# Recurrent attention and a GELU layer: v cast by its DMA, the first loads let go in another order, and a newly searched list of steps

## The chip, the cores and the metric

The kernel runs on one core of a Trainium2 chip. The metric is device time in microseconds of one execution; lower is better. The engines are named as the profile names them: PE (TensorE, matrix products; PEld is its weight loads), DVE (VectorE), ACT (ScalarE), POOL (GpSimd) and SP (SyncE). [...]

## The reference

First a gated recurrence, for 4 batches, 8 heads, 768 steps and a head size of 48, then a dense layer with a GELU in the middle over all 3072 tokens:

```python
for t in range(S):
    state = alpha[:, :, t, :, None] * state + np.einsum('bhd,bhe->bhde', k[:, :, t], v[:, :, t])
    y[:, :, t] = np.einsum('bhd,bhde->bhe', q[:, :, t], state)
x = y.transpose(0, 2, 1, 3).reshape(B * S, H * D)          # 3072 x 384
h = x @ w_in                                               # 384 x 2048
g = 0.5 * h * (1.0 + np.tanh(c * (h + 0.044715 * h * h * h)))
out = g @ w_out                                            # 2048 x 384
```

Inputs and output are float32.

## The kernel before, in words

**Tiling.** The 768 steps are cut into 6 chunks of 128. A *unit* is one chunk of one batch: 128 rows of 8 heads by 48, which is 384 columns. A *pair* is two units of the same chunk, batches 0 and 1 or 2 and 3. Pairs 0 to 11 run in order of time; pairs 0 and 1 are both of the first chunk and carry no state in. A step of pair m is named by its kind, the pair, and a number: `kp0.0` is the first `kp` of pair 0.

**Attention of one pair.** `ln` takes the logarithm of alpha (ACT). `cum` sums it over the rows by products with a triangle of ones (PE). `b` and `binv` are the exponentials of plus and minus the sums, `bend` that of the total (ACT). `qp` = q times b and `kp` = k times binv (DVE, line 460). `t` turns qp or kp by PE products with the identity, and `ev` copies the turned tile out (DVE or ACT). `attn` is k times q (PE, line 552), `mask` cuts it to the lower triangle (DVE, line 571), `y` multiplies by v (PE). `x` copies y out, `tx` turns it, `xe` copies it into xT, the input of layer 1. `kv` and `st` make the next state. In pairs 0 and 1 (`PACKED`) the rows of alpha, q and k lie in memory order of another shape, so kp must be turned back for `kv`: those are `t0.4`, `t0.5`, `t1.4` and `t1.5`, with an `ev` each.

**Dense layers.** Layer 1 of one pair is eight blocks `l1m.n`, each of six products of 128 x 256 columns into one bank of PSUM (line 658), each followed by a `gelu` (ACT). Layer 2 (`l2m.n`) is four steps of four products for each unit (line 677), then `ot` copies the result out and `store` sends it (SP).

**Loads.** The rows of pairs 0 and 1 come by twelve *ring loads* of 192 KB on the hardware queues, load.0 to load.11 in the order of `RINGS`; `BY_ACT` says which of them ACT issues, SP issues the rest. POOL issues everything else in the order of `LOADS`: v of pairs 0 and 1 (load.12 and load.14 before), the parts of W_in and W_out, and the rows of later pairs. A `gate` is a small POOL copy that waits for a load and so holds back what POOL issues behind it (line 352). For the pairs in `NARROW`, v comes as float32 and is cast to bf16 by `vb` (line 427); for the others the DMA casts.

**What sets the order.** A scheduler in the kernel holds one list of steps for all engines, `FIRST`. Each entry names an engine and a step (P is PE, V is DVE, A is ACT, G is POOL, S is SP). Each engine runs its own entries strictly in the order of the list; a step waits for what it needs, and all behind it on that engine wait too. `P:fill.n` puts n products of zeros on PE (line 327). `LANDED` holds times at which the scheduler takes the first loads to have landed, by name of the load; it enters no instruction. Tiles come from pools with a fixed number of buffers (`BUFS`): four banks `ff` for layer 1, layer 2 and the sums of pairs 0 and 1, two `yk` for turned tiles, y and kv.

Of the kernel before, what the change touches and what calls it, by code (L numbers as in the profile page):

```python
# [171 lines left out]
class _Kernel:  # L172
# [9 lines left out]
    BY_ACT = (2, 3,)

    FIRST = """
        A:table.0 A:load.2 A:load.3 S:load.0 S:load.1 S:load.4 A:ln0.0 S:load.5 P:fill.7 P:cum0.0 A:ln0.1 G:gate.0 G:load.12 S:load.6 P:cum0.1 A:b0.0
# [2 lines left out]
        P:fill.1 P:t0.4 V:ev0.4 P:fill.1 P:attn0.1 A:ln1.0 G:load.15 P:t0.5 V:mask0.3 P:cum1.0 A:ev0.5 G:load.16 V:vb0.0 A:ln1.1 P:y0.0 V:mask0.2
        G:load.17 P:kv0.0 A:binv1.0 P:cum1.1 V:st0.0 A:x0.0 G:load.18 A:vb0.1 V:kp1.0 P:tx0.0 A:b1.0 P:y0.1 V:xe0.0 G:load.19 V:qp1.0 P:t1.1 A:x0.1
        A:bend1.0 G:load.20 A:b1.1 P:fill.1 P:t1.0 A:ev1.0 V:ev1.1 G:load.21 V:qp1.1 P:fill.1 P:kv0.1 V:st0.1 G:load.22 A:binv1.1 A:bend1.1 P:tx0.1  # L190
        P:attn1.0 V:xe0.1 G:load.23 G:load.24 G:load.25 G:load.26 P:t1.2 P:l10.0 V:kp1.1 V:mask1.0 V:mask1.1 G:load.27 G:load.28 P:t1.3 A:ev1.2
        A:ev1.3 V:vb1.0 P:l10.1 P:t1.4 P:attn1.1 P:y1.0 A:gelu0.0 A:gelu0.1 V:ev1.4 P:l10.2 P:l10.3 A:gelu0.2 P:l10.4 P:t1.5 A:ev1.5 V:vb1.1 V:x1.0
        P:l10.5 V:mask1.2 V:mask1.3 P:y1.1 V:x1.1 P:tx1.0 A:gelu0.3 V:xe1.0 P:l10.7 A:gelu0.4 A:gelu0.7 G:load.29 G:load.30 G:load.31 G:load.32
        P:tx1.1 V:xe1.1 A:gelu0.5 P:l10.6 P:l11.0 A:gelu0.6 P:l11.4 P:l11.3 P:l11.5 A:gelu1.0 A:gelu1.4 A:gelu1.3 P:l11.2 A:gelu1.5 A:gelu1.2 P:l11.7
        A:gelu1.7 P:l11.1 P:l11.6 A:gelu1.1 P:l20.0 A:ln2.0 P:l20.3 P:l20.7 P:cum2.0 P:kv1.0 P:l20.11 P:l20.4 A:b2.0 A:binv2.0 A:ln2.1 P:cum2.1 A:b2.1
        V:st1.0 V:kp2.0 V:qp2.0 P:kv1.1 V:st1.1 G:load.33 G:load.34 G:load.35 G:load.36 G:load.37 V:qp2.1 P:l20.1 G:load.38 P:l20.5 P:l20.8 A:binv2.1
        V:kp2.1 A:gelu1.6 V:tr2.0 V:tr2.1 P:t2.0 A:ev2.1 V:ev2.0 V:tr2.2 V:tr2.3 P:l20.12 G:load.39 G:load.40 G:load.41 G:gate.2 G:load.42 G:gate.3
        G:load.43 G:gate.4 G:load.44 A:ot0.0 P:l20.15 P:attn2.0 A:ot0.3 P:l20.2 V:mask2.2 V:mask2.3 P:l20.9 P:l20.6 A:ln3.0 P:cum3.0 A:b3.0 V:mask2.0
        V:mask2.1 P:y2.0 P:l20.13 V:x2.0 P:y2.1 A:x2.1 V:qp3.0 P:l20.10 P:tx2.0 A:binv3.0 P:tx2.1 A:ot0.1 V:xe2.0 V:xe2.1 P:l20.14 A:ot0.2 P:kv2.0
        V:kp3.0 P:l12.6 P:l12.0 A:gelu2.0 A:gelu2.6 P:l12.5 V:st2.0 P:t3.0 A:gelu2.5 P:l12.1 A:ev3.1 V:tr3.0 P:l12.3 V:tr3.1 V:ev3.0 P:kv3.0 P:l12.7  # L200
        P:kv2.1 A:gelu2.1 P:l12.4 A:gelu2.7 A:gelu2.3 A:gelu2.4 P:l12.2 V:tr3.2 P:l22.4 V:tr3.3 V:st3.0 V:st2.1 P:attn3.0 A:gelu2.2 P:l22.5 P:l22.6
        V:mask3.2 V:mask3.3 A:ln4.0 P:cum4.0 P:l22.0 A:ln5.0 V:mask3.0 V:mask3.1 A:b4.0 P:y3.0 P:l22.7 A:x3.0 P:y3.1 P:kv3.1 V:qp4.0 P:l22.1 A:binv4.0
        A:x3.1 P:l22.2 A:ot2.1 P:tx3.1 V:st3.1 S:store0.0 V:tr4.0 V:xe3.1 P:cum5.0 P:tx3.0 V:xe3.0 V:kp4.0 P:l22.3 P:l13.0 A:binv5.0 A:b5.0 A:ot2.0
        P:l13.3 S:store0.3 P:t4.0 V:tr4.1 V:tr4.2 V:tr4.3 S:store2.1 V:ev4.0 P:l13.4 P:l13.2 V:ev4.1 P:kv4.0 A:gelu3.0 A:gelu3.3 A:gelu3.2 A:gelu3.4
        P:l13.5 A:gelu3.5 G:gate.5 G:load.45 G:gate.6 G:load.46 G:gate.7 G:load.47 G:gate.8 G:load.48 G:gate.9 G:load.49 G:gate.10 G:load.50 G:gate.11
        G:load.51 G:gate.12 G:load.52 G:gate.13 G:load.53 G:gate.14 G:load.54 G:gate.15 G:load.55 G:gate.16 G:load.56 G:gate.17 G:load.57 G:gate.18
        P:kv4.1 P:l13.6 P:l13.1 A:gelu3.6 P:l13.7 V:st4.0 V:st4.1 P:attn4.0 A:gelu3.1 P:l23.0 P:l23.1 A:gelu3.7 S:store2.0 S:store0.1 V:qp5.0 V:tr5.0
        A:ln6.0 V:mask4.2 V:mask4.0 V:mask4.3 V:mask4.1 V:kp5.0 P:l23.2 P:y4.0 P:l23.3 V:ot3.0 S:store3.0 P:y4.1 A:x4.0 A:x4.1 P:cum6.0 P:l23.4 A:b6.0
        P:tx4.0 V:xe4.0 P:tx4.1 V:xe4.1 P:l23.5 A:binv6.0 V:qp6.0 P:t5.0 A:ev5.1 A:ln7.0 V:ev5.0 P:l23.6 P:l23.7 P:attn5.0 P:l14.0 A:ot3.1 V:tr6.0
        V:tr5.1 V:tr5.2 V:mask5.0 S:store0.2 P:l14.4 P:l14.3 V:mask5.1 A:gelu4.0 A:gelu4.4 S:turn6.0 P:l14.6 S:store3.1 A:gelu4.3 A:gelu4.6 V:mask5.2  # L210
        V:mask5.3 P:y5.0 A:x5.0 V:kp6.0 V:tr6.1 V:tr6.2 P:l14.5 V:tr5.3 P:l14.2 A:gelu4.5 A:gelu4.2 P:y5.1 P:l14.1 A:gelu4.1 P:l14.7 P:kv5.1 V:x5.1
        V:tr6.3 P:kv5.0 A:gelu4.7 P:l24.0 P:cum7.0 A:b7.0 A:binv7.0 V:st5.1 P:l24.4 V:st5.0 P:kv6.0 S:turn6.1 V:st6.0 V:qp7.0 P:l24.5 P:l24.1 P:l24.2
        A:ln8.0 P:tx5.0 P:tx5.1 P:cum8.0 V:xe5.1 V:xe5.0 V:kp7.0 A:binv8.0 P:l24.3 V:ot4.0 P:l24.6 A:b8.0 P:l24.7 A:ot4.1 P:attn6.0 V:mask6.0 P:l15.0
        V:mask6.1 P:l15.2 P:l15.4 P:l15.5 V:mask6.2 V:kp8.0 V:mask6.3 P:y6.0 A:gelu5.0 A:gelu5.2 A:gelu5.4 P:l15.6 P:l15.1 V:x6.0 A:gelu5.6 A:gelu5.5
        P:y6.1 V:qp8.0 A:x6.1 S:turn7.0 P:l15.3 P:kv6.1 P:l15.7 A:gelu5.1 P:l25.4 S:turn7.1 P:l25.0 A:gelu5.3 P:l25.5 P:l25.6 A:gelu5.7 A:ln9.0
        V:st6.1 P:attn7.0 P:l25.1 V:mask7.2 P:l25.7 V:mask7.3 G:load.58 G:gate.19 G:load.59 G:gate.20 G:load.60 S:turn6.2 P:l25.2 A:ot5.1 V:mask7.0
        P:cum9.0 A:binv9.0 G:gate.21 G:load.61 G:gate.22 V:mask7.1 V:tr8.0 P:l25.3 P:y7.0 P:y7.1 P:l16.0 V:ot5.0 V:tr7.0 V:tr7.1 A:gelu6.0 A:x7.0
        P:l16.5 P:l16.7 P:l16.3 V:x7.1 S:store4.0 S:turn8.0 P:kv8.1 P:kv8.0 A:gelu6.7 A:gelu6.5 A:gelu6.3 S:turn7.2 V:tr8.1 V:tr8.2 P:l16.6 A:gelu6.6
        P:l16.4 A:gelu6.4 P:l16.1 P:l16.2 A:gelu6.1 A:gelu6.2 V:tr8.3 V:st8.1 V:st8.0 V:tr7.2 V:tr7.3 P:kv7.1 V:st7.1 V:kp9.0 P:kv7.0 P:l26.0 P:l26.1
        P:l26.4 P:l26.5 P:l26.2 S:turn8.1 A:ln10.0 A:b9.0 V:tr9.0 V:tr9.1 V:tr9.2 V:tr9.3 G:load.62 G:gate.23 G:load.63 G:gate.24 G:load.64 G:gate.25  # L220
        V:qp9.0 P:cum10.0 A:binv10.0 P:l26.3 P:l17.0 P:l26.6 P:l26.7 A:ot6.0 A:b10.0 S:turn9.1 A:gelu7.0 P:l17.6 A:gelu7.6 V:ot6.1 V:st7.0 P:l17.1
        A:gelu7.1 P:l17.2 P:l17.3 A:gelu7.2 P:attn8.0 S:turn9.0 V:mask8.0 V:mask8.1 A:gelu7.3 P:l17.7 P:l17.4 A:gelu7.4 A:gelu7.7 P:l17.5 V:mask8.2
        A:gelu7.5 P:l27.0 G:load.65 P:y8.0 V:mask8.3 A:x8.0 P:l27.4 P:y8.1 P:l27.5 P:l27.6 P:l27.1 V:x8.1 V:qp10.0 P:kv9.0 V:kp10.0 A:ln11.0 P:cum11.0
        A:binv11.0 A:b11.0 P:l27.7 P:l27.2 S:turn8.2 P:l27.3 S:store4.1 V:st9.0 P:attn9.0 V:kp11.0 S:store5.1 V:qp11.0 A:ot7.0 A:ot7.1 S:turn10.1
        P:l18.0 S:turn10.0 A:gelu8.0 S:store6.1 P:l18.3 V:mask9.0 V:mask9.1 P:l18.1 A:gelu8.1 A:gelu8.3 P:l18.7 P:l18.5 V:mask9.2 S:turn11.1 V:mask9.3
        P:y9.0 P:y9.1 V:x9.0 V:x9.1 S:store6.2 S:store5.0 S:store6.0 S:turn9.2 S:store7.0 A:gelu8.7 A:gelu8.5 P:l18.2 A:gelu8.2 S:store6.3 P:l18.4
        A:gelu8.4 P:attn10.0 V:mask10.2 V:mask10.3 V:mask10.0 P:l18.6 P:l28.0 P:l28.1 V:mask10.1 A:gelu8.6 P:l28.2 P:l28.3 P:y10.0 P:l19.0 S:store7.3
        S:turn11.0 A:x10.0 A:gelu9.0 P:l19.6 A:gelu9.6 P:y10.1 V:ot8.0 V:x10.1 P:kv9.1 V:st9.1 S:store7.1 P:l19.5 P:l19.3 A:gelu9.5 A:gelu9.3 P:l19.1
# [807 lines left out]
```

## Time and profile before

| | |
|---|---|
| median of 3 runs | 174.1 us (173.99 to 174.16) |
| the profiled execution | 173.77 us |
| its span, first to last instruction | 171.9 us |
| PE busy | 166.3 us (97%) |
| ACT busy | 125.5 us (73%) |
| DVE busy | 107.7 us (63%) |
| POOL busy | 63.0 us (37%) |
| DMA | 29.40 MB, mean 171 GB/s |

Times in the profile are microseconds from the first instruction. A row of a timeline gives the start, the time taken, the engine, the line, the operation and the tiles, with "xN" where N instructions follow each other; the bracket tells how long the engine had been idle and what released it. The chain that ended last is followed back from the last instruction, at each step to what released it. A row of DMA issues gives the tiles, the issuing queue, the count, the size and the median time from issue to landing.

### The profile page before, as it was taken

The page shows a single profiled execution, that of the slowest core. Times are in us where ns is not written, and L with a number is a line of the kernel's source. Part 1 is how long each engine was busy: PE and PEld are TensorE (multiplying, and loading weights), DVE is VectorE, ACT ScalarE, POOL GpSimd, SP SyncE. Part 2 cuts the span into 40 slices and gives each one's busy share as a digit, 9 for nine tenths or more (in the row PEclk, how much of TensorE's full clock was granted, in tenths as well). Part 3 has the DMA queues.
Part 4 walks back from the last instruction along what each step waited for, and adds up shares of the span by engine and source line. Part 5 has one row for each costly group of instructions (what it writes and reads, how often), then busy time and mean ns, then how long its engine had stood idle before and what let it go on. Part 6 is the DMA issues. An engine that isn't in the chain of part 4 may idle for free.

```text
span 171.9 us, 4595 instructions
## 1 busy us (share of the span) xinstructions
PE 166.3 (97%) x1909; PEld 129.8 (75%) x1909; DVE 107.7 (63%) x210; ACT 125.5 (73%) x205; POOL 63.0 (37%) x88
## 2 busy tenths in 40 slices
PE   7999999999999999999999999999999999999991
PEld 2566899666886896797697797796797978987860
DVE  6499820588978999998892898865947550100100
ACT  4578889897999798899779499868882636651412
...
GB/s 138 311 268 217 199 247 230 231 230 228 256 208 96 257 218 241 169 165 242 145 224 213 158 226 138 181 233 60 232 186 148 147 1 114 4 0 40 101 48 92
DMA packets 51541, 29.40 MB, mean 171 GB/s; under 512 B 39616, under 2 KB 47936, under 8 KB 51520
## 3 DMA queue, kind: packets, MB, share of 16 engines
...
q14 instruction: 6, 0.05, 0.1%
...
## 4 chain that ended last, share of the span: by engine, by line
PE 91%; DMA 3%; ACT 3%; DVE 0%; issue 0%; DVEq 0%
PE hT L658 37%; PE acc L677 37%; PE at L552 4%; DMA k<-in_k_dram 3%; PE yps L627 2%; PE cum L416 2%; PE kv L581 2%; PE qkT_ps L484 1%; PE xT_ps L646 1%; PE qkT_ps L470 1%; PE yps L561 1%; ACT qkT L508 1%; PE k_ps L516 1%; ACT L318 1%; PE idle L327 1%; PE yps L617 1%
## 5 line engine op out<-in xcount | busy, mean ns | idle before, releaser
L658 PE MATMUL hT<-xT,w_in 128*128 128x256 bf16 x576 | 69.4, 273 | 0.0
L677 PE MATMUL acc<-w_out,gT 128*128 128x384 bf16 (+3 forms) x416 | 68.9, 314 | 0.0
L664 ACT ACTIVATE gT<-hT 128x512 bf16<-128x512 f32 x96 | 53.6, 600 | 15.2 <-PE hT L658 13.1
L658 PEld LDWEIGHTS <-w_in 128*128 128x128 bf16 x576 | 60.6, 114 | 1.2 <-DMA w_in<-in_moe_w_in_dram 0.3
L677 PEld LDWEIGHTS <-gT 128*128 128x128 bf16 x416 | 37.4, 98 | 20.2
L571 DVE TENSOR_TENSOR atm<-at,ut 128x512 bf16<-128x512 f32 x48 | 30.1, 683 | 8.2 <-PE at L552 8.0
L689 DVE COPY ot<-acc 128x384 f32<-128x384 f32 (+2 forms) x9 | 4.3, 488 | 20.0 <-PE acc L677 20.0
L689 ACT COPY ot<-acc 128x384 f32<-128x384 f32 (+1 forms) x17 | 7.9, 472 | 11.6 <-PE acc L677 9.3
L595 DVE STREAM_TRANSPOSE tr<-b 32x256 f32<-32x256 f32 x32 | 14.0, 438 | 1.4 <-ACT b L449 0.8
L346 POOL DMA_DIRECT2D k<-in_k_dram x11 | 12.2, 1111 | 5.7 <-DMA v<-in_v_dram 1.7
L346 POOL DMA_DIRECT2D a<-in_alpha_dram x11 | 12.3, 1117 | 4.4 <-issue 1.7
L460 DVE TENSOR_TENSOR qp<-q,b 128x768 bf16<-128x768 f32 (+1 forms) x15 | 11.9, 792 | 2.8 <-ACT b L449 2.6
L346 POOL DMA_DIRECT2D vb<-in_v_dram x11 | 12.2, 1105 | 3.6 <-issue 1.9
L346 POOL DMA_DIRECT2D q<-in_q_dram x11 | 12.2, 1112 | 2.5 <-DMA w_out<-in_moe_w_out_dram 1.0
L449 ACT ACTIVATE binv<-cum 128x768 bf16<-128x768 f32 (+1 forms) x15 | 10.1, 684 | 3.3 <-PE cum L416 3.3
L460 DVE TENSOR_TENSOR kp<-k,binv 128x768 bf16<-128x768 f32 (+1 forms) x15 | 11.9, 791 | 0.5 <-ACT binv L449 0.5
L318 ACT ACT_TABLE_LOAD x9 | 11.5, 1283 | 0.9 <-PEq L1020 0.7
L449 ACT ACTIVATE b<-cum 128x768 f32<-128x768 f32 (+1 forms) x15 | 10.3, 685 | 2.0 <-PE cum L416 1.5
L664 ACT ACT_TABLE_LOAD x9 | 11.5, 1283 | 0.2
L606 DVE TENSOR_TENSOR stmp<-kv,st 128x384 f32<-128x384 f32 x16 | 8.9, 555 | 1.9 <-PE kv L581 1.2
L608 DVE TENSOR_TENSOR st<-stmp,tr 128x384 bf16<-128x384 f32 x16 | 8.9, 558 | 0.6
L399 ACT ACTIVATE la<-a 128x768 f16<-128x768 f32 (+1 forms) x11 | 8.5, 784 | 0.1
...
## 6 DMA issues: line engine op xcount, KB each, us to landing
out_dram<-ot SPq DMA_DIRECT2D x19, 192.0 KB, 3.0
...
vb<-in_v_dram POOLq DMA_DIRECT2D x9, 192.0 KB, 6.3
...
w_out<-in_moe_w_out_dram POOLq DMA_DIRECT2D x4, 384.0 KB, 11.0
...
```

The source lines that it names most:

```text
L318: nc.scalar.add_instruction(mybir.InstLoadActFuncSet(name=nc.get_next_instruction_name(), act_func_set_id=i, engine=mybir.EngineType.Activ ...
L346: dma(u[t][:, lo:hi].rearrange("t b h d -> t (b h) d"), src.rearrange("b h s d -> s (b h) d")[c * C:(c + 1) * C])
L449: self.nc.scalar.activation(u[n].rearrange("t i h d -> t i (h d)")[:, lo:hi], cum, AF.Exp, scale=1.0 if n == "b" else -1.0)
L460: self.nc.vector.tensor_tensor(out, rows, b, op=ALU.mult)
L571: self.nc.vector.tensor_tensor(u["atm", i][:, o], u["at", i][o], self.ut[:, None, :].to_broadcast([self.C, self.H // 2, self.C]), op=ALU.mult)
L595: self.nc.vector.transpose(u["tr"][f:f + 32, :, 0:32], rows[:, lo:lo + H * 2 * D].rearrange("t (g n) -> t g n", n=2 * D)[:, :, 0:32])
L606: nc.vector.tensor_tensor(s, acc, old, op=ALU.add)
L608: nc.vector.tensor_tensor(new, acc, end[:, :, None].to_broadcast([C, H // 2, 2 * D]), op=ALU.mult)
L658: self.nc.tensor.matmul(h[:, s].rearrange("p (g t) -> p g t", t=self.C), w_in[:, j, nt % 4 + s], self.xT[c % self.NX][:, lo:hi, j], start= ...
L664: return lambda e: self.nc.scalar.activation(self.gT[c % self.NG][:, nt:nt + 2, lo * self.C:hi * self.C], f.pop(("h", c, lo, nt)), AF.Gelu ...
L677: self.nc.tensor.matmul(f["acc", c, b][:, lo:hi], self.gT[c % self.NG][:, nt, b * self.C:(b + 1) * self.C], self.w_out[:, nt, lo:hi], star ...
L689: self.copy(e)(f["ot", c, b][:, sl], f["acc", c, b] if half is None else f["acc", c, b, half][:, sl])
```

## The change

Five things are edited.

- `NARROW` is empty: v of pairs 0 and 1 comes as bf16 from its DMA, and the four `vb` casts are gone.
- `RINGS` swaps two entries, so that load.4 is now k and load.5 q of pair 0, unit 1. `BY_ACT` leaves load.2 alone to ACT. `LOADS` lets POOL go on from the alpha of pair 0, unit 0 (it was unit 1), drops the gate on k, and puts W_in 1 ahead of the second v.
- `APART`: four of the eight layer-1 blocks of pair 0 (nt 0, 2, 4, 6) are done for one unit first (`h1`, six products of 128 columns) and then for the other.
- Layer 2 no longer has to come after all layer-1 blocks of the first two pairs (`firsts`).
- `FIRST` is a new list from its first entry, and `LANDED` has new times. In the new list 7 products of zeros are left of 17. The ring loads stand in it as A: load.2 and S: load.0, 1, 8, 5, 7, 9, 10, 4, 6, 3, 11.

The edits around `u["apart"]` in `cum` and `exp` are for pairs that take `ff` banks without being packed; there are none.

```diff
-    LOADS = ('gatea 0 1', 'v0', 'gatek 0 1', 'in 0', 'v1', 'in 1', 'in 2', 'in 3', 'out 0', 'out 1', '2a', 'out 2', '2b', 'out 3', '3', '4', '5', 'win3', '6', '7', '8', '9', '10', '11')
+    LOADS = ('gatea 0 0', 'v0', 'in 0', 'in 1', 'v1', 'in 2', 'in 3', 'out 0', 'out 1', '2a', 'out 2', '2b', 'out 3', '3', '4', '5', 'win3', '6', '7', '8', '9', '10', '11')
...
-    RINGS = (('a', 0, 0, 1), ('a', 0, 1, 2), ('q', 0, 0, 1), ('k', 0, 0, 1), ('q', 0, 1, 2), ('k', 0, 1, 2),
+    RINGS = (('a', 0, 0, 1), ('a', 0, 1, 2), ('q', 0, 0, 1), ('k', 0, 0, 1), ('k', 0, 1, 2), ('q', 0, 1, 2),
              ('a', 1, 0, 1), ('a', 1, 1, 2), ('q', 1, 0, 1), ('k', 1, 0, 1), ('q', 1, 1, 2), ('k', 1, 1, 2))
-    BY_ACT = (2, 3,)
+    BY_ACT = (2,)
...
-        A:table.0 A:load.2 A:load.3 S:load.0 S:load.1 S:load.4 A:ln0.0 S:load.5 P:fill.7 P:cum0.0 A:ln0.1 G:gate.0 G:load.12 S:load.6 P:cum0.1 A:b0.0
-        S:load.7 A:bend0.0 V:qp0.0 A:binv0.0 A:binv0.1 S:load.8 V:kp0.0 P:fill.2 P:t0.0 A:b0.1 V:ev0.0 P:fill.1 P:t0.1 S:load.9 A:ev0.1 V:qp0.1
-        S:load.10 A:bend0.1 P:fill.3 P:attn0.0 V:kp0.1 G:gate.1 S:load.11 P:t0.2 G:load.13 V:mask0.0 A:ev0.2 P:t0.3 G:load.14 V:mask0.1 A:ev0.3
...
+        A:table.0 A:load.2 S:load.0 P:fill.7 A:ln0.0 P:cum0.0 S:load.1 S:load.8 S:load.5 S:load.7 A:ln0.1 A:b0.0 G:gate.0 S:load.9 V:qp0.0 A:binv0.0
+        S:load.10 G:load.12 S:load.4 S:load.6 S:load.3 G:load.13 G:load.14 G:load.15 G:load.16 G:load.17 G:load.18 G:load.19 G:load.20 P:cum0.1 A:b0.1
+        P:t0.0 V:kp0.0 A:ln1.0 A:binv0.1 P:t0.1 P:cum1.0 V:ev0.0 V:qp0.1 P:t0.2 V:kp0.1 A:bend0.1 A:bend0.0 A:ev0.1 P:attn0.0 V:ev0.2 A:b1.0 A:binv1.0
+        V:mask0.0 V:mask0.1 P:t0.3 A:ev0.3 P:attn0.1 V:mask0.2 P:y0.0 A:bend1.0 A:ln1.1 A:x0.0 P:cum1.1 S:load.11 P:tx0.0 V:qp1.0 P:t1.0 A:ev1.0
+        A:bend1.1 A:binv1.1 A:b1.1 V:kp1.0 V:xe0.0 V:mask0.3 P:t1.1 V:ev1.1 P:h10.0 P:y0.1 P:h10.3 P:t1.4 P:attn1.0 A:x0.1 P:tx0.1 P:h10.1 A:ev1.4
...
+        P:l211.2 P:l211.3 V:ot11.0 S:store11.0 P:l211.7 P:l211.8 P:l211.9 A:ot11.1 A:ot11.2 A:ot11.3 S:store9.0 S:store11.1 S:store11.3 S:store8.1
+        S:store11.2 P:l210.0 P:l210.4 P:l210.5 P:l210.6 P:l210.7 P:l210.1 V:ot10.1 S:store9.1 S:store10.1 P:l210.2 P:l210.3 A:ot10.0 S:store10.0
...
-    NARROW = (0, 1)
+    NARROW = ()
...
+    APART = (0, 2, 4, 6)
...
-    def layer1(self, f, c, lo, hi, nt):
+    def layer1(self, f, c, lo, hi, nt, units=None):
+        a, b = units or (lo, hi)
...
-                    self.nc.tensor.matmul(h[:, s].rearrange("p (g t) -> p g t", t=self.C), w_in[:, j, nt % 4 + s],
-                                          self.xT[c % self.NX][:, lo:hi, j],
+                    self.nc.tensor.matmul(h[:, s, (a - lo) * self.C:(b - lo) * self.C].rearrange("p (g t) -> p g t", t=self.C), w_in[:, j, nt % 4 + s],
+                                          self.xT[c % self.NX][:, a:b, j],
...
-                t = s.add("l1", {"PE": W["l1_4"]}, 10000 + n, self.layer1(f, c, lo, hi, nt),
-                          [xts[c, b] for b in range(lo, hi)] + [loads["w", "in", nt // 4]], stream=n - 16 if m > 1 else None)
+                h1 = []
+                if m == 0 and nt in self.APART:
+                    h1 = [s.add("h1", {"PE": W["l1_2"]}, 10000 + n, self.layer1(f, c, lo, hi, nt, (lo, lo + 1)), [xts[c, lo], loads["w", "in", nt // 4]])]
+                t = s.add("l1", {"PE": W["l1_2" if h1 else "l1_4"]}, 10000 + n, self.layer1(f, c, lo, hi, nt, (lo + 1, hi) if h1 else None),
+                          [xts[c, b] for b in range(lo, hi)] + [loads["w", "in", nt // 4]] + h1, stream=n - 16 if m > 1 else None)
...
-                          gs[m if m else b // 2][2 * part:2 * part + 2] + [loads["w", "out", min(part, 3)]] + firsts, stream=n - 16)
+                          gs[m if m else b // 2][2 * part:2 * part + 2] + [loads["w", "out", min(part, 3)]], stream=n - 16)
```

More of the change, by code (lines that the diff above doesn't have):

```diff
@@ L181 @@
              ('a', 1, 0, 1), ('a', 1, 1, 2), ('q', 1, 0, 1), ('k', 1, 0, 1), ('q', 1, 1, 2), ('k', 1, 1, 2))
-    BY_ACT = (2, 3,)
+    BY_ACT = (2,)
     FIRST = """
-        A:table.0 A:load.2 A:load.3 S:load.0 S:load.1 S:load.4 A:ln0.0 S:load.5 P:fill.7 P:cum0.0 A:ln0.1 G:gate.0 G:load.12 S:load.6 P:cum0.1 A:b0.0
-        S:load.7 A:bend0.0 V:qp0.0 A:binv0.0 A:binv0.1 S:load.8 V:kp0.0 P:fill.2 P:t0.0 A:b0.1 V:ev0.0 P:fill.1 P:t0.1 S:load.9 A:ev0.1 V:qp0.1
-        S:load.10 A:bend0.1 P:fill.3 P:attn0.0 V:kp0.1 G:gate.1 S:load.11 P:t0.2 G:load.13 V:mask0.0 A:ev0.2 P:t0.3 G:load.14 V:mask0.1 A:ev0.3
[L188 to L228, printed above, removed]
-        S:store8.0 S:turn10.2 A:gelu9.1 P:attn11.0 V:mask11.2 V:mask11.3 P:l19.2 A:gelu9.2 V:mask11.0 V:mask11.1 P:l28.4 P:l28.5 P:l28.6 P:l28.7
-        A:ot8.1 P:y11.1 P:l19.4 P:y11.0 P:l19.7 A:x11.0 A:gelu9.4 A:gelu9.7 V:x11.1 P:l110.0 S:store8.1 P:l110.4 S:turn11.2 S:store7.2 P:l110.3
-        A:gelu10.0 A:gelu10.4 A:gelu10.3 P:l29.4 P:l29.5 P:l29.6 P:l110.2 P:l29.7 V:ot9.1 A:gelu10.2 P:l111.0 P:l111.5 A:gelu11.0 A:gelu11.5 P:l111.7
-        P:l111.3 P:l111.2 P:l111.1 A:gelu11.7 A:gelu11.3 P:l111.6 A:gelu11.2 A:gelu11.1 P:l111.4 P:l211.0 P:l211.1 A:gelu11.4 P:l211.2 A:gelu11.6
-        P:l211.4 P:l211.5 A:ot11.1 P:l211.3 A:ot11.0 P:l211.6 P:l211.7 P:l29.0 P:l29.1 P:l29.2 P:l211.8 P:l29.3 P:l211.9 S:store11.1 V:ot11.2
-        S:store11.2 P:l110.6 V:ot9.0 S:store9.0 P:l110.1 A:gelu10.6 V:ot11.3 S:store11.3 S:store11.0 A:gelu10.1 P:l110.7 P:l110.5 S:store9.1
-        A:gelu10.7 P:l210.4 P:l210.5 P:l210.0 P:l210.1 A:gelu10.5 P:l210.6 P:l210.2 P:l210.7 A:ot10.1 P:l210.3 A:ot10.0 S:store10.1 S:store10.0
@@ new lines @@
+        A:gelu0.5 P:tx1.0 V:xe1.0 G:load.25 G:load.26 G:load.27 G:load.28 P:l10.7 P:tx1.1 P:l10.6 V:xe1.1 A:gelu0.4 A:gelu0.7 A:gelu0.6 P:l11.0
+        P:l11.4 G:load.29 G:load.30 G:load.31 G:load.32 G:load.33 G:load.34 G:load.35 G:load.36 P:l11.7 P:l11.5 P:t1.5 P:t0.5 A:gelu1.0 G:load.37
+        G:load.38 G:load.39 G:load.40 A:gelu1.7 A:gelu1.4 A:gelu1.5 P:l11.1 A:gelu1.1 P:l11.3 A:gelu1.3 P:l11.2 A:gelu1.2 V:ev0.5 V:ev1.5 P:kv1.0
+        P:kv1.1 A:ln2.0 A:ln2.1 V:st1.0 P:l20.0 P:l20.4 V:st1.1 P:kv0.0 V:st0.0 P:kv0.1 V:st0.1 P:l11.6 P:cum2.0 P:l20.8 P:l20.3 A:b2.0 A:binv2.0
@@ L415, in emit @@
                     continue
-                nc.tensor.matmul(cum[:, i, 0:H * D], self.ut_h, la[:, i, :, 0:D], start=True, stop=True)
+                rows = cum[lo] if u["apart"] else cum[:, i]
+                nc.tensor.matmul(rows[:, 0:H * D], self.ut_h, la[:, i, :, 0:D], start=True, stop=True)
                 for p in range(H // 2) if u["sums"] == "PE" else ():
-                    nc.tensor.matmul(cum[:, i, H * D + p:H * D + p + 1],
+                    nc.tensor.matmul(rows[:, H * D + p:H * D + p + 1],
                                      la[:, i, 2 * p:2 * p + 2, :].rearrange("t h d -> t (h d)"),
@@ L447, in emit @@
                     u[n] = self.sb.tile([self.C, 2, H, D], BF16, tag=n, bufs=self.BUFS["binv"], name=n)
-                cum = u["cum"][lo][:, None, 0:H * D] if u["packed"] else u["cum"][:, lo:hi, 0:H * D]
+                cum = u["cum"][lo][:, None, 0:H * D] if u["apart"] else u["cum"][:, lo:hi, 0:H * D]
                 self.nc.scalar.activation(u[n].rearrange("t i h d -> t i (h d)")[:, lo:hi], cum, AF.Exp,
@@ L749, in tasks @@
         for step in self.LOADS:
-            if step[0] == "v":
-                rows(int(step[1:]), "v")
+            if step[0] in "aqkv" and step[1:].isdigit():
+                rows(int(step[1:]), step[0])
             elif step[:4] == "gate":
@@ L801, in tasks @@
             if m in self.CUM_FF:
-                cums[0].take("ff", *exps[:3])
-                cums[1].take("ff", *exps[3:])
+                cums[0].take("ff", *exps[:len(exps) // 2])
+                cums[1].take("ff", *exps[len(exps) // 2:])
             else:
                 cums[0].take("ca", *exps)
-            if m in self.SPLIT:
+            if m in self.SPLIT and m not in self.CUM_FF:
                 cums[1].deps += exps[:2]
@@ L927, in tasks @@
         n = 0
-        f, gs, l2s, ots, parts_of, firsts = {}, {}, {}, [], [], []
+        f, gs, l2s, ots, parts_of = {}, {}, {}, [], []
         def layer1(m):
```

52 lines of the change are left out of this document (46 added, 6 removed), and 9 rows, old and new, of the table LANDED.

## The prediction

> **What bounds the kernel now.** I read the page's busy shares and slices first, then the chain that ended last, then the first microseconds of SP's, TensorE's and VectorE's timelines, then the DMA issues of that stretch.
>
> ```profile
> PE 166.3 (97%) x1909; PEld 129.8 (75%) x1909; DVE 107.7 (63%) x210; ACT 125.5 (73%) x205; POOL 63.0 (37%) x88
> ...
> PE   7999999999999999999999999999999999999991
> ```
>
> TensorE is the bound from the second slice to the last. But its busy time counts products of zeros (line 327), so the early nines are not all work. The chain, in order of time (start, length, what):
>
> ```profile
> 1.92 5.28 DMA k<-in_k_dram
> ...
> 7.29 0.57 DVE kp L460
> ...
> 16.95 0.66 PE hT L658 x6
> ...
> 23.61 5.90 PE hT L658 x54
> ```
>
> Up to 16.8 us the chain is one of latency: it waits for the k rows of pair 0, unit 0 (load.3) until 7.20, and goes through the first pair's attention. From the first layer-1 product on, TensorE has work without a break; beyond 30 us the starts of its products leave only three waits over 0.1 us that are no change of tile shape (at 37.4, 52.5 and 107.5), 0.46 us together. So the time is: when the first layer-1 product starts, plus the TensorE work still undone then, plus a fixed end (last product 168.3, copy 0.48, store, 171.9).
>
> What lets load.3 land at 7.20 is where it stands among the ring loads. SP's issues, then what the issues of 0.7 to 2.0, of 4.9 to 6.1 and of 7.3 to 8.3 us took to land:
>
> ```profile
> 0.73 1.41 SPq L343 DMA_DIRECT2D a<-in_alpha_dram  x2
> 2.20 0.61 SPq L343 DMA_DIRECT2D q<-in_q_dram  x1
> 2.85 0.62 SPq L343 DMA_DIRECT2D k<-in_k_dram  x1
> 3.52 1.27 SPq L343 DMA_DIRECT2D a<-in_alpha_dram  x2
> 4.83 0.61 SPq L343 DMA_DIRECT2D q<-in_q_dram  x1
> 5.49 0.61 SPq L343 DMA_DIRECT2D k<-in_k_dram  x1
> ```
>
> ```profile
> a<-in_alpha_dram SPq DMA_DIRECT2D x2, 192.0 KB, 3.1
> ...
> k<-in_k_dram ACTq DMA_DIRECT2D x1, 192.0 KB, 5.3
> ```
>
> ```profile
> k<-in_k_dram SPq DMA_DIRECT2D x1, 192.0 KB, 5.9
> ```
>
> ```profile
> q<-in_q_dram SPq DMA_DIRECT2D x1, 192.0 KB, 4.5
> k<-in_k_dram SPq DMA_DIRECT2D x1, 192.0 KB, 4.3
> ```
>
> SP issues one load per 0.65 us. The first two landed 3.1 us after issue, those in a backlog 4.3 to 5.9. load.3 was the second issue of ACT's own queue, at 1.92.
>
> **The change, part by part.**
>
> *Ring loads in another order.* In the new list SP issues load.0, 1, 8, 5, 7, 9, 10, 4, 6, 3, 11; ACT only load.2. So load.3 goes from the fourth ring load to the eleventh. SP's first eight issues start at 0.73 to 5.49 as above; the ninth follows at 6.14 and load.3 at 6.80. It lands between 6.80 + 3.05 = 9.85 (an empty queue) and 6.80 + 5.9 = 12.7 (the tenth of before, which met the first v on POOL's queue). I take 11.9: the eleventh of before landed at 7.42 + 4.5 = 11.9, and POOL's loads are no less in the way here, since the new gate waits for the first alpha (3.8) instead of the second (4.8), and the gate on k (POOL idle for 1.80 us until it) is gone, so v0 and W_in are let go up to 3 us earlier, among the ring loads.
>
> Who waits: kp0.0 is VectorE's second product. Behind it on VectorE stand ev0.0, qp0.1, kp0.1 and everything else; on TensorE t0.1, its transpose, stands before the cumulative sums of pair 1 and all that follows. Only cum0.0, cum0.1 and t0.0 go ahead. So kp0.0 moves from 7.29 to 11.9, +4.6 us. load.6 (alpha of pair 1) is issued just before it and lands just before it; the others earlier.
>
> *The new order behind kp0.0.* Before, the first layer-1 product came 9.5 us after kp0.0 (16.79). Now VectorE carries the path: kp .47, ev .60, qp .47, kp .47, ev .60, three masks at .605, qp .47, kp .47 (start to start, from VectorE's timeline), 5.4 us with a short wait; then xe and a transpose of k, 0.6: the first product at 11.9 + 6.05 = 17.95. From there to the first block of pair 1 TensorE has eight layer-1 blocks (8 x .655), three y (.20 each), four transposes (.22), two attn (.33), three tx (.17): 7.9, and 0.2 of waits. That block starts at 26.05; before it started at 23.61 + .66 = 24.27: +1.8. Not done by then, though done before: t0.5, t1.5, kv0.0, kv0.1: 2 x .22 + 2 x .17 = +0.8. Together +2.6.
>
> *Products of zeros.* Ten of 17 go. They stood in waits, 0.22 us each, and cost nothing in the sum above. But without them, and with load.3 late, TensorE stands idle from 6.6 to 12.5. What that does to its pace no row of before shows; these are the nearest:
>
> ```profile
> 1.19 3.17 PE L327 MATMUL idle<-zero 128*128 128x512 bf16 x7 [1.19 <-DVE ones L990]
> 4.37 1.39 PE L384 MATMUL cum<-la,ut_blk 128*128 128x384 f16 x7
> ...
> 5.70 0.82 PE L384 MATMUL cum<-la,ut_blk 128*128 128x384 f16 x7
> ```
>
> After standing, TensorE took 0.42 us from one 512-column product to the next, and started the first cum0 at half pace too, until about 4.9, 3.7 us after its first product; later the same product took 0.22. The granted clock of the page reads full throughout and does not tell the two apart. If TensorE falls back to that pace, t0.1 (.22), cum1.0 (.76) and t0.2 (.22) cost 1.2 us more, of which 1.1 reaches ev0.2 and the masks behind it, and 0.4 follows with t0.3 and attn0.1: +1.5. Ends: 0 (it keeps its pace) and +2.4 (half pace up to the first layer-1 product). I take +1.5: the start of this kernel, a stand followed by sparse work, is the row it is nearest to. [...]
>
> *v cast by DMA.* Four casts go (three of 0.35 on VectorE, one of 0.53 on ACT). On VectorE they were in the latency stretch, which I have counted anew without them. The casting load writes 192 KB in 96-byte pieces; later loads of this kind landed 1.4 to 2.2 us after the one before them, the uncast a, q and k 1.8: -0.4 to +0.4 on POOL's queue. y0.0 needs v0 at 15.9, 4 us after the latest landing I can make of it (it is first of POOL's queue): 0. W_in 0 is needed at 17.95; before it landed at 14.3, two places later on POOL: 0. If the rings were fast again, W_in would be next.
>
> *Four blocks by units.* 48 products of 128 columns (.056 each) take the place of 24 of 256 (.109): +0.07 in all, within the 0.2 of waits.
>
> *The rest of the list; removed dependencies.* The waits beyond 30 us may go or others come: -0.5 to +0.5; I take -0.3, most of the 0.46 us of waits above, whose places the new order does not repeat; the end (l210.3, ot10.0, store10.0) is the same. The edits in cum and exp change no instruction for pairs 0 and 1.
>
> Sum against the profiled execution: 173.77 + 2.6 + 1.5 - 0.3 = 177.6. The median of the runs, 174.1, is 0.3 above it: 177.9.
>
> **The rivals.** A change under 0.2% (0.35 us) can't be told from none here.
>
> *Late k, full pace* (+2.3): 176.4. For it: in all the trace the pace never fell once it was up. Against: there was no stand over 0.5 us in which it could.
>
> *k early.* If the ring loads run at 0.56 us each without losing to POOL's queue, load.3 lands at 9.85 to 10.5: +0.2 to +0.9, around 174.9. For it: SP's loads landed 0.5 to 0.6 us apart from 7.4 to 9.6. Against: the next took 1.8 us more once v0's packets ran.
>
> *Faster.* The shortening behind kp0.0 (9.5 to 6.05 us, less the 0.8 put off) is worth some 2 us if load.3 does not pay for it. The point that decides is its landing: no loss at 9.6, a gain before. At 9.0 the time is 173.5. Against: that is 2.2 us after its issue, and no ring load landed in under 3.0.
>
> *The order does not hold* (SP issuing load.3 early after all) would give 7.3 and 171.8; the instructions stand in the listed order, so it keeps 0.01.
>
> **How the numbers follow.** Late k and half pace 0.50 (177.9), late k at full pace 0.28 (176.4), k early 0.14 (174.9; a third of it within 0.2%), faster 0.07, and 0.01 for the last. The likeliest, by itself, runs from 176.3 (landing 11.0) to 179.8 (13.2, with half pace up to layer 1). The range reaches down through the second and into the third case: 175.2 to 179.8, leaving some 0.12 below and 0.06 above. Faster 0.08, same 0.05, slower 0.87.
>
> **What would show it.** The chain of the changed kernel should begin with a DMA of k until about 11.9, from SP, not ACT; TensorE idle from 6.6 to 12.5 in front of the transposes of kp; transposes and sums behind it at twice their spacing if the pace fell; the first layer-1 product near 18 to 19.5; no wait for W_in behind it. A k that lands before 9.6 would make the forecast wrong, and so would long TensorE waits after 30 us.

## The result and the profile after

| | before | changed |
|---|---|---|
| median | 174.10 us (3 runs) | 183.49 us (182.93 to 184.04, 4 runs) |
| the profiled execution | 173.77 us | 183.54 us |
| its span | 171.9 us | 181.8 us |

The changed kernel takes 1.054 times as long, with a 95% interval of 1.050 to 1.058. The forecast was slower, at 177.9 us in a range of 175.2 to 179.8. So the sign came out, and the chain that was forecast, but the size did not: the time lies 3.7 us above the range. Executions that took over 1.5% longer than the fastest of their kernel are left out of all comparisons, and as the profiles of the two runs named "v uncast" and "old loads, new list" below are of such executions, only their first 30 and 20 us are read.

First the busy shares, the slices of TensorE and the slices of the granted clock of the changed kernel (40 slices of 4.5 us):

```profile
PE 165.7 (91%) x1923; PEld 131.3 (72%) x1923; DVE 112.0 (62%) x215; ACT 120.7 (66%) x196; POOL 62.3 (34%) x87
...
PE   7501899999999999999999999999999999999992
...
PEclk9955569999999999999999999999999999999999
```

TensorE is busy for about as long (165.7 us against 166.3; ten products of zeros fewer, and part of the work at a slower pace) in a span that is 9.9 us longer, and the gap is in the second to fifth slice. Behind them the slices are full, as before. In the third to fifth slice the clock shows 5, which is half, and in the sixth 6. In the kernel before, that row was full throughout:

```profile
PEclk9999999999999999999999999999999999999999
```

The start of the chain that ended last (start, length, what):

```profile
6.84 9.80 DMA k<-in_k_dram
...
16.73 0.57 DVE kp L463
...
17.35 0.61 PE qkT_ps L473 x4
...
25.31 0.59 PE hT L665 x6
```

It is the chain that was forecast: the k rows of pair 0, unit 0 (load.3), issued by SP at 6.84, hold back kp0.0, then t0.1, then cum1.0. But load.3 landed at 16.64, where the forecast had 11.9. TensorE's timeline shows the stand in front of t0.1 and where layer 1 begins:

```profile
17.35 0.61 PE L473 MATMUL qkT_ps<-ident,kp 128*128 128x128 bf16 x4 [10.09 <-DVE kp L463]
17.75 1.49 PE L386 MATMUL cum<-la,ut_blk 128*128 128x384 f16 x7
...
25.10 0.79 PE L665 MATMUL hT<-xT,w_in 128*128 128x128 bf16 x6
```

Busy time of the engines and granted clock in four stretches (PEclk is the column in front of the DMA share):

```profile
core 0: us, PE busy (x) PEld busy (x) DVE busy (x) ACT busy (x) POOL busy (x), PEclk, DMA share, GB/s
0.00:7.00 7.00, 5.35 (x32) 2.70 (x33) 3.26 (x21) 3.58 (x6) 4.28 (x13) 1.00 0.64 185
7.00:17.00 10.00, 0.25 (x4) 0.08 (x2) 0.27 (x1) 1.03 (x4) 5.30 (x7) 0.58 1.41 212
17.00:25.50 8.50, 7.46 (x73) 5.72 (x74) 6.45 (x13) 3.77 (x10) 3.77 (x5) 0.50 1.32 211
25.50:30.00 4.50, 4.50 (x86) 4.20 (x85) 4.10 (x8) 3.80 (x7) 2.26 (x4) 0.98 1.30 234
```

From 17 to 25.5 us everything on TensorE ran at half its clock. The cumulative sum at 17.75 took 1.49 us; before, the same form took 0.82 at 5.70.

The 9.77 us between the two profiled executions, 5.94 of which the sum of the prediction (177.6) did not have, split into three:

| stretch | forecast | measured | off by |
|---|---|---|---|
| kp0.0 starts | 11.9 | 16.73 | 4.83 |
| from kp0.0 to the first layer-1 product | 6.05 + 1.5 = 7.55 | 25.10 - 16.73 = 8.37 | 0.82 |
| from there to the end, more than before | 1.44 - 0.3 = 1.14 | (183.54 - 25.10) - (173.77 - 16.79) = 1.46 | 0.32 |

(The three add up to the 5.94 to rounding. 1.44 is the +2.6 of the late k less the 17.95 - 16.79 = 1.16 by which the first layer-1 product was to move.) What had to be explained was chiefly the 4.8 us of the landing.

### The profile page after: what moved, and what is told of

Read it like the earlier page. It is cut to its first block, busy times and chain, and to the rows that moved or that the text cites. A ratio compares the mean times of both kernels' runs of the same rounds, so it can differ in the third digit from the quotient of the medians.

```text
span 181.8 us, 4611 instructions
## 1 busy us (share of the span) xinstructions
PE 165.7 (91%) x1923; PEld 131.3 (72%) x1923; DVE 112.0 (62%) x215; ACT 120.7 (66%) x196; POOL 62.3 (34%) x87
## 4 chain that ended last, share of the span: by engine, by line
PE 88%; DMA 5%; SPq 3%; ACT 1%; issue 0%; DVE 0%; DVEq 0%
PE hT L665 35%; PE acc L684 35%; DMA k<-in_k_dram 5%; PE at L555 4%; SPq L345 3%; PE yps L630 2%; PE cum L419 2%; PE kv L584 2%; PE qkT_ps L473 2%; PE cum L386 1%; PE xT_ps L649 1%; PE qkT_ps L487 1%; PE yps L564 1%; PE yps L620 1%; PE k_ps L519 0%
## 5 line engine op out<-in xcount | busy, mean ns | idle before, releaser
L665 PE MATMUL hT<-xT,w_in 128*128 128x256 bf16 (+1 forms) x600 | 69.7, 270 | 0.0
L665 PEld LDWEIGHTS <-w_in 128*128 128x128 bf16 x600 | 61.8, 114 | 1.1
L696 DVE COPY ot<-acc 128x384 f32<-128x384 f32 x13 | 7.2, 557 | 21.9 <-PE acc L684 21.3
L463 DVE TENSOR_TENSOR kp<-k,binv 128x768 bf16<-128x768 f32 (+1 forms) x15 | 11.9, 793 | 10.7 <-DMA k<-in_k_dram 9.9
L348 POOL DMA_DIRECT2D vb<-in_v_dram x13 | 14.6, 1122 | 4.1 <-issue 2.6
L696 ACT COPY ot<-acc 128x384 f32<-128x384 f32 (+3 forms) x13 | 5.6, 431 | 13.1 <-PE acc L684 12.3
L348 POOL DMA_DIRECT2D k<-in_k_dram x11 | 12.2, 1111 | 5.9 <-DMA w_out<-in_moe_w_out_dram 2.2
L348 POOL DMA_DIRECT2D a<-in_alpha_dram x11 | 12.2, 1113 | 5.8 <-DMA vb<-in_v_dram 2.1
L348 POOL DMA_DIRECT2D q<-in_q_dram x11 | 12.2, 1108 | 5.2 <-DMA w_in<-in_moe_w_in_dram 2.1
L463 DVE TENSOR_TENSOR qp<-q,b 128x768 bf16<-128x768 f32 (+1 forms) x15 | 11.9, 794 | 3.2 <-ACT b L452 3.1
L640 DVE CAST x<-yps 128x384 bf16<-128x384 f32 x11 | 6.0, 557 | 9.0 <-PE yps L630 5.3
L473 PE MATMUL qkT_ps<-ident,kp 128*128 128x128 bf16 x16 | 2.2, 283 | 10.1 <-DVE kp L463 10.1
```

Source lines behind the costliest of these rows:

```text
L348: dma(u[t][:, lo:hi].rearrange("t b h d -> t (b h) d"), src.rearrange("b h s d -> s (b h) d")[c * C:(c + 1) * C])
L463: self.nc.vector.tensor_tensor(out, rows, b, op=ALU.mult)
L665: self.nc.tensor.matmul(h[:, s, (a - lo) * self.C:(b - lo) * self.C].rearrange("p (g t) -> p g t", t=self.C), w_in[:, j, nt % 4 + s], self ...
L696: self.copy(e)(f["ot", c, b][:, sl], f["acc", c, b] if half is None else f["acc", c, b, half][:, sl])
```

## The experiments

The theory: the place of load.3 in SP's queue costs what was forecast, and the rest of its delay comes from POOL's loads, which now start before the rings are done; the stand of TensorE costs more because the clock falls. Rivals: the ring order is harmless and POOL's traffic alone does it; or the new list is slower in itself; or the casting loads with their 96-byte pieces are to blame.

"Changed" below is the changed kernel; diffs are against it unless said otherwise. Of long lists the entries that move are shown; a gate's own entry in the list, and the loads that stand behind it, move to match and are not shown. The kernel before ran again beside each set of runs, and the ratios are to those.

| run | ratio to before (95%) | load.3 lands | first layer-1 product |
|---|---|---|---|
| changed | 1.054 (1.050 to 1.058) | 16.64 | 25.10 |
| ring order undone | 1.015 (1.010 to 1.021) | 6.57 | 17.09 |
| gate on k behind v0 | 1.041 (1.033 to 1.049) | 13.04 | 21.50 |
| zeros in the stand | 1.041 (1.035 to 1.046) | 16.11 | 22.45 |
| v uncast | 1.094 (1.079 to 1.108) | 19.41 | 29.00 |
| k by ACT | 1.012 (0.997 to 1.026) | 6.96 | 14.17 |
| old loads, new list | 1.012 (0.999 to 1.026) | 6.95 | 14.50 |
| old list, cast | 1.000 (0.995 to 1.006) | 7.04 | 16.84 |
| old list, new ring order | 1.027 (1.011 to 1.044) | 12.36 | 24.11 |
| POOL behind k | 1.024 (1.020 to 1.028) | 10.85 | 18.32 |
| W_in 0 first | 1.006 (1.001 to 1.010) | 7.04 | 15.20 |
| W_in 0 first, zeros | 1.003 (1.000 to 1.007) | 7.37 | 15.76 |

**The ring order undone.** SP issues its ring loads in the order of their numbers; all else is as in the changed kernel.

```diff
- S:load.0 S:load.1 S:load.8 S:load.5 S:load.7 S:load.9 S:load.10 S:load.4 S:load.6 S:load.3 S:load.11
+ S:load.0 S:load.1 S:load.3 S:load.4 S:load.5 S:load.6 S:load.7 S:load.8 S:load.9 S:load.10 S:load.11
```

> The changed kernel with SP's ring loads let go in the order of their numbers (load.0, 1, 3, 4, 5, 6, 7, 8, 9, 10, 11); nothing else differs. Theory (late k of pair 0, and the half clock behind the stand that it makes, are the whole loss): load.3 lands near 6.5, kp0.0 goes at 6.6 to 7.3 as before the change, and what is late next are the q and k of pair 1 (issues 8 and 9 of SP, 13 and 15 us); the first layer-1 product comes near 16.5 and the time is 172.5 to 175.5 us. Rival (the new list or the early weights are slow in themselves, the late k costs little): 180 us or more.

176.68 us (176.30 to 177.12). Undoing the order gives back 6.8 of the 9.4 us, so most of the loss needs it, but that is 1.2 us less than expected. The chain shows what is late next:

```profile
6.14 9.59 DMA k<-in_k_dram
...
15.83 0.56 DVE kp L460
...
17.29 0.64 PE hT L662 x6
```

This k is load.9, of pair 1, unit 0. It has the same fate as load.3 had: issued at 6.14, landed at 15.73, and kp1.0 stands ahead of xe0.0 on VectorE, so layer 1 waits for it. Issued at 6.14 here and at 6.84 in the changed kernel, a ring load took 9.59 and 9.80 us to land.

**A gate on k behind v0.** POOL issues v0, then waits for load.3 before it issues W_in.

```diff
-    LOADS = ('gatea 0 0', 'v0', 'in 0', 'in 1', 'v1', ...
+    LOADS = ('gatea 0 0', 'v0', 'gatek 0 0', 'in 0', 'in 1', 'v1', ...
```

> The changed kernel with one gate more: behind v0 POOL waits for load.3 (k of pair 0, unit 0) before it lets W_in go. Ring order as changed. Theory (W_in's 1024-byte pieces take turns with the ring loads' 768-byte pieces, one for one, from 9 us on, and so hold load.3 back): load.3 lands at 11 to 12.5 instead of 16.6, the stand is 2 to 4 us shorter at least, and the time is 177 to 179.5 us. Rival (the 96-byte pieces of the casting load of v hold it back): they are still there, so load.3 lands at 15.5 or later and the time is 182 us or more.

181.44 us, and load.3 at 13.04: without W_in beside the rings it lands 3.6 us earlier, but later than expected. The time is 2 us above what was expected. From kp0.0 (13.13) to the first layer-1 product it took 8.4 us, as in the changed kernel, so the half clock was paid in full (the sum at 14.15 took 1.49 us); and behind that product the profiled execution takes 2.0 us longer than the changed kernel, of which 1.2 is one wait of TensorE, up to 93.2 us, for a DMA that turns qp (`qkT<-qp`); what held up that DMA stays open. W_in is the larger share of what delays load.3 (3.6 us), v0 a smaller one.

**POOL behind k altogether.** The one gate of POOL waits for load.3 in place of alpha, so that nothing of POOL runs beside the rings.

```diff
-    LOADS = ('gatea 0 0', 'v0', ...
+    LOADS = ('gatek 0 0', 'v0', ...
```

> The changed kernel, ring order as changed, but POOL's one gate waits for load.3 (k of pair 0, unit 0) and not for the first alpha, so that neither v0 nor W_in runs beside the ring loads. Theory (its place as SP's tenth issue costs load.3 only some 3 us behind its issue at 6.8; all above that is POOL's traffic, which takes turns with SP's queue): load.3 lands at 9.9 to 10.8 instead of 16.6, and W_in, let go 5 us later, becomes the late one; 176 to 182 us. Rival (SP's queue is slow by itself with eleven loads in it): load.3 lands at 12 or later.

178.46 us, as expected. Its chain starts so:

```profile
6.79 4.06 DMA k<-in_k_dram
...
10.91 0.18 POOL gate L351
```

load.3 lands at 10.85, 2.2 us before the run with v0 alone beside it. So of its delay against before (7.20), 3.65 us belong to its place in SP's queue, and 5.8 us to POOL's traffic. The DMA queues between 7 and 9 us show the second part directly (packets, MB, and the time that the packets took as a share of 16 engines, 140.7% in one of the rows). First this run, then the changed kernel:

```profile
q1 hardware_dynamic: 777, 0.56, 94.3%
```

```profile
q0 software_dynamic: 1532, 0.15, 140.7%
q1 hardware_dynamic: 278, 0.20, 35.9%
```

q1 is SP's queue, q0 POOL's. Beside the 96-byte pieces of v0 SP moved 0.20 MB instead of 0.56. Then W_in comes on. The changed kernel between 12 and 15 us:

```profile
q0 software_dynamic: 404, 0.39, 77.9%
q1 hardware_dynamic: 404, 0.29, 39.4%
```

404 pieces of one queue beside 404 of the other: while W_in ran, SP got about one piece of 768 bytes for each of POOL's of 1024 (some twenty on each side are shorter). That is 97 GB/s, from which a load of 192 KB is estimated at 2.0 us. The ring loads of the changed kernel landed at 10.63, 13.04, 15.06, 16.64 and 17.60, so 2.4, 2.0, 1.6 and 1.0 us apart, where the four before them were 0.5 us apart (6.48, 7.03, 7.53, 8.04). What the expectations call taking turns is, as measured, these equal counts beside W_in; in what order the two queues were served was not shown. Beside v0 the counts, 1532 and 278, are far from equal, and no run here shows why.

**v uncast.** v of pairs 0 and 1 comes as float32, with the four casts on VectorE; all else is as in the changed kernel.

```diff
-    NARROW = ()
+    NARROW = (0, 1)
...
+ V:vb0.0 V:vb0.1 V:vb1.0 V:vb1.1
```

> The changed kernel with v of pairs 0 and 1 loaded as float32 and cast by VectorE (four casts ahead of the y that needs each). Theory (W_in's turns hold load.3 back, not the cast of v): load.3 lands within 1.5 us of 16.6 and the time is 182.5 to 185 us. Rival (the 96-byte pieces do it): load.3 lands by 13.5 and the time is 180.5 us or less.

190.3 us, and load.3 at 19.41, 2.8 us later than in the changed kernel instead of within 1.5 (read from one profile). That misses the expectation, and goes against the rival still more: the casting loads are not what is wrong. The queues between 7 and 9 us:

```profile
q0 software_dynamic: 91, 0.35, 61.0%
q1 hardware_dynamic: 286, 0.21, 35.7%
```

Beside 91 large pieces of uncast v SP moved 0.21 MB, as it moved 0.20 beside the 1532 small ones, and v brings twice the bytes. In this order of loads v cast by DMA is even the better choice (1.054 against 1.094). Part of the longer time lies behind the landing: the casts stand in front of y0.0 and y0.1 here, with waits of TensorE of 1.05 and 0.41 us for them. The first layer-1 product came 3.9 us later than in the changed kernel, which the 2.8 and the 1.05 make up.

**The cast alone.** The kernel before with the casting loads, and the four `vb` gone from its list (the diff is against before).

```diff
-    NARROW = (0, 1)
+    NARROW = ()
...
- V:vb0.0 A:vb0.1 V:vb1.0 V:vb1.1
```

> The kernel before with one part of the change: v of pairs 0 and 1 cast by DMA, the four casts of VectorE and ACT left out of the list. Theory (the cast itself is hidden): the ring loads land within 0.7 us of before, and the time is 173.3 to 174.6 us. Rival (the casting load's 96-byte pieces hold the ring loads back): k of pair 1 lands 1 us or more later, and the time is 174.8 us or more.

174.86 us, 1.000 (0.995 to 1.006). By the figures alone this is the rival's: the time lies 0.3 us above the theory's range, and the last three ring loads moved from 11.39, 11.88 and 12.32 to 9.89, 12.29 and 13.46, so the last k of pair 1 came 1.1 us later. But the kernel before took 174.73 us beside it, so a ratio of 1.000 is what counts: with the old list and the old gates, any cost of the cast is below 0.6%.

**The ring order alone.** The kernel before with SP's order of the change and load.3 on SP, POOL's gates as they were (the diff is against before, the loads called by the numbers that they have there).

```diff
-    BY_ACT = (2, 3,)
+    BY_ACT = (2,)
...
- S:load.0 S:load.1 S:load.4 S:load.5 S:load.6 S:load.7 S:load.8 S:load.9 S:load.10 S:load.11
+ S:load.0 S:load.1 S:load.8 S:load.4 S:load.7 S:load.9 S:load.10 S:load.5 S:load.6 S:load.3 S:load.11
```

> The kernel before with one part of the change: SP issues the ring loads in the changed order (k of pair 0, unit 0 tenth), ACT only the first q; the gates stay, so W_in waits for the eighth load of SP. Theory (the order alone makes most of the loss): load.3 lands at 11 to 13.5, the clock falls in the stand, and the time is 178 to 182 us. Rival (the order needs the early W_in to do harm): load.3 lands by 10.5 and the time is below 177 us.

180.79 us (180.14 to 181.22), within what the theory had set. Its chain:

```profile
6.79 5.57 DMA k<-in_k_dram
...
12.45 0.57 DVE kp L457
```

With the gate on k kept, load.3 lands at 12.36, near the 11.9 of the prediction. (That gate waits for the k of unit 1, which the new order puts at 11.31 instead of 7.92, so W_in is let go later too, at 11.91 instead of 8.52; TensorE did not wait for it.) kp0.0 starts 5.2 us later than in the kernel before, and the profiled execution takes 7.0 us more; the clock was at half from 12.5 to 19.3 us. So the order by itself is worth some 5 to 7 us of loss in the old list too; the ratio, 1.027, says 4.8 us, and its interval allows 1.9 to 7.6.

**Zeros in the stand.** 45 products of zeros in front of t0.1 keep TensorE busy while it waits for load.3.

```diff
- P:t0.0 V:kp0.0 A:ln1.0 A:binv0.1 P:t0.1
+ P:t0.0 V:kp0.0 A:ln1.0 A:binv0.1 P:fill.45 P:t0.1
```

> The changed kernel with 45 products of zeros on TensorE ahead of t0.1, 9.7 us of them at full pace, so that TensorE does not stand while k is late. Theory (the half clock is a cost of its own, worth about 2.4 us): the granted clock stays full, load.3 lands at 16.6 as before, the first layer-1 product comes about 6 us behind kp0.0 instead of 8.4, and the time is 180.5 to 181.7 us. Rival (the late k is all of it, and the half clock lies beside VectorE's work): 183 us or more.

181.02 us (180.70 to 181.62), as the theory had it. TensorE's timeline, and the same stretch as above:

```profile
17.08 0.39 PE L470 MATMUL qkT_ps<-ident,kp 128*128 128x128 bf16 x4
17.30 0.82 PE L383 MATMUL cum<-la,ut_blk 128*128 128x384 f16 x7
...
22.45 0.50 PE L662 MATMUL hT<-xT,w_in 128*128 128x128 bf16 x6
```

```profile
17.00:25.50 8.50, 7.41 (x129) 6.16 (x127) 8.16 (x16) 5.87 (x14) 3.96 (x5) 1.00 1.32 210
```

The clock stays at 1.00, and from t0.1 to the first layer-1 product it takes 5.37 us instead of 7.75: the half clock costs 2.4 us. (The time falls by as much, but load.3 also landed 0.5 us earlier here, and the zeros held t0.1 up by 0.3.) From kp0.0, at 16.20, it is 6.25 us, beside the 6.05 that the prediction had counted for full pace.

**k by ACT.** load.3 goes back to ACT's queue, and SP issues the rest in the order of numbers; POOL starts as early as in the changed kernel.

```diff
-    BY_ACT = (2,)
+    BY_ACT = (2, 3,)
...
+ A:load.3
- S:load.8 S:load.5 S:load.7 S:load.9 S:load.10 S:load.4 S:load.6 S:load.3 S:load.11
+ S:load.4 S:load.5 S:load.6 S:load.7 S:load.8 S:load.9 S:load.10 S:load.11
```

> The changed kernel with SP's ring loads in the order of their numbers and load.3 issued by ACT behind load.2, as before the change; POOL's early loads stay. Theory (W_in's pieces take turns one for one with SP's queue, so what counts is how many ring loads are still out when they begin at 9 us): one load less on SP, so the k of pair 1, unit 0 (the last that the first layer-1 product needs) lands 2 us earlier than with all eleven on SP (there 15.7), at 13.2 to 14.2, and the time is 174 to 175.7 us. Rival (the order on SP was all of it, and what is left over 174.1 is the new list): the same time as with all on SP, 176.2 to 177.2 us.

177.43 us (176.79 to 179.14): a miss, no better than the ring order undone. load.3 landed at 6.96 and the k of pair 1, unit 0 at 12.84, even earlier than expected, but now W_in 1, at 16.89, is what TensorE waits for.

**Old loads, new list.** As the last one, and POOL's two gates and their places as in the kernel before. The new list, the halved blocks, the cast, the freed layer 2 and the swap of load.4 and load.5 are left of the change.

```diff
-    LOADS = ('gatea 0 0', 'v0', 'in 0', ...
+    LOADS = ('gatea 0 1', 'v0', 'gatek 0 1', 'in 0', ...
```

> The changed kernel with the ring order, ACT's two loads and POOL's two gates of before; v is still cast by its DMA, the list and the layer-1 halves are the new ones. Theory (the new list is the shorter one, and only the landings spoil it): ring loads land as before (load.3 7.2, k of pair 1 11.4), W_in 0 near 14.3, the first layer-1 product near 14.5 and the time 171.3 to 173.2 us, faster than before. Rival (the new list is slow in itself): 174 us or more.

178.17 us (176.93 to 178.97), a clear miss: the new list with the old loads is not faster than the old list. TensorE's timeline:

```profile
14.50 0.53 PE L662 MATMUL hT<-xT,w_in 128*128 128x128 bf16 x6 [0.41 <-DMA w_in<-in_moe_w_in_dram]
...
17.72 0.53 PE L662 MATMUL hT<-xT,w_in 128*128 128x128 bf16 x6 [2.50 <-DMA w_in<-in_moe_w_in_dram]
```

The first layer-1 product does come 2.3 us earlier than in the kernel before (14.50 to 16.79). But the second block in the list is `h10.3`, which reads another quarter of W_in, and that landed at 17.67.

**W_in 0 first, without and with zeros.** The last kernel with the blocks that read W_in 0 put first (two steps of ACT, x0.1 and gelu0.3, move with them); the second of the two also has ten products of zeros in four places.

```diff
- P:h10.0 P:y0.1 P:h10.3 ... P:tx0.1 P:h10.1 ... P:t1.2 P:h10.2 P:t1.3 P:l10.1 P:l10.3 P:t0.4 P:l10.0 ... P:l10.2
+ P:h10.0 P:y0.1 P:h10.1 ... P:tx0.1 ... P:t1.2 P:t1.3 P:l10.0 P:l10.1 P:h10.3 P:h10.2 P:l10.3 P:t0.4 ... P:l10.2
```

> The new list with the ring order, ACT's loads and POOL's gates of before, and one edit in the list: the four layer-1 products sets that read W_in 0 go ahead of those that read W_in 1, which landed at 17.7 there and held all of TensorE for 2.7 us. Theory (W_in 1 is what is late next): the wait goes to other work, and the time falls by 0.8 to 2 us against that kernel's fast runs (176.9 to 179), to 175 to 176.5 us. Rival (the half clock of the stretch makes the time): no more than 0.4 us faster.

> The same with ten products of zeros put back in four waits (ahead of attn0.0, of the first sums of pair 1, of t1.0 and of the first layer-1 set). Theory (the new list lost its pace for want of them): the granted clock stays full and the time is 172.8 to 174.5 us, 1 to 2.5 us below the same without zeros. Rival (the clock falls by less work than zeros can make up, or it lies beside VectorE's work): within 0.5 us of the same without zeros.

175.08 us (12 runs) and 174.90 us (11 runs), 1.006 and 1.003 times the kernel before. The wait for W_in 1 is gone. The median fell by 3.1 us with it, but the ratio only from 1.012 to 1.006, which lies within the interval of the first, so how much the wait was worth is not clear. The zeros held the clock at 1.00 and yet brought no more than 0.2 us, a tenth of what was hoped for. In the second run TensorE, idle from 15.5, still waited for W_in 0 in front of the first layer-1 product:

```profile
15.76 0.53 PE L662 MATMUL hT<-xT,w_in 128*128 128x128 bf16 x6 [0.24 <-DMA w_in<-in_moe_w_in_dram]
```

No version came out faster than the kernel before. The new list in itself is therefore no gain, and with these loads no great loss either. Why it is not faster with early k and without the wait for W_in 1 stays open in part. The traces show where to look: up to 30 us TensorE was busy for 27.99 us in the kernel before, and for 26.10 and 26.00 us in these two. The earlier first layer-1 product (15.20 and 15.76 instead of 16.79) came with more standing of TensorE around it, 3.9 and 4.0 us instead of 2.0, and not with less.

## Why the prediction was wrong in size, and where it was right

*The landing of load.3: the step that failed.* "I take 11.9: the eleventh of before landed at 7.42 + 4.5" carried a landing over from a list in which a gate on k kept W_in back until 8.52. The very next clause said that the gate was gone and that "v0 and W_in are let go up to 3 us earlier, among the ring loads", and set no price on it. With the gate the assumption holds (12.36 in the run with the ring order alone); with POOL's loads kept wholly behind, the landing is 10.85; without a gate, 16.64. The upper end of 12.7 was taken from a ring load that had met one v, and the eleventh of before, besides its v, had met W_in only at its end: from 11.0 to 11.9 us POOL's queue moved 109 pieces beside SP's 166. The forecast asked of W_in only whether it would land late for its own users; it does not (15.30, first used at 25.10). Its harm was what it did to the queue beside it. This is 4.8 of the 5.9 us.

*The half pace: right in kind, mis-sized.* It was taken at 1.5 with an upper end of 2.4 for half pace up to the first layer-1 product; the zeros show 2.4. That the pace would fall at all was the author's estimate from the start of the kernel before: its row of the clock is full throughout and shows no fall. In the place of that estimate the changed kernel showed a fall, to a granted clock of 0.50. The longer stand (10.1 us, not 5.9) took the clock no lower than that, but it came back late: it fell at 8.63 us and was full again only at 25.70, 8.3 us after work resumed. The stretches at half in these traces are multiples of 3.41 us: 17.07 us here, five of them; 3.41 with POOL behind k, 6.83 with the ring order undone and 13.65 with the gate on k: one, two and four (mean granted clocks of the profiled executions: 0.953, 0.990, 0.977 and 0.962). In the last three lengths of 3.41 us before 25.70 TensorE was busy for 45%, 80% (a wait of 0.68 us at 20.85 lies in it) and 99%, and only behind the full one did the clock return. In the 3.41 us before the fall, from 5.22 to 8.63, TensorE was busy for 1.62 us (47%). One statement on the profile was wrong: the prediction said that the granted clock of the page does not tell the two paces apart. In the first 5 us it does not (1.00 throughout), but here the row of the clock shows 5 in three slices.

*The waits after 30 us.* -0.3 was taken for them, and nothing was gained; 0.3 us.

*Right.* The chain begins with a DMA of k from SP; TensorE stands in front of the transposes of kp; sums and transposes behind took about twice their time (1.49 us beside 0.82, 0.61 beside 0.40); the way from kp0.0 to layer 1 at full pace (6.05 forecast, 6.25 with zeros); the work from the first layer-1 product to the end (+1.44 forecast without the -0.3, +1.46 measured); the cast by DMA costs nothing that the runs could tell (1.000). "If the rings were fast again, W_in would be next" came out three times (k by ACT, old loads, POOL behind k).

*The rivals.* Late k at full pace is refuted by the clock (0.50), k early by the landing (16.64). The rival "faster" valued the shorter way behind kp0.0 at some 2 us if load.3 does not pay for it. With load.3 at 7 us that gain did not come, as W_in took over: TensorE waited for it until 16.89 with k by ACT and until 17.67 with the old loads. The prediction took a stand of over 0.5 us as what the pace needs to fall; the last section shows it falling over three waits of 0.42, 0.47 and 0.73 us.
